# V of layer A transposed as pairs of bf16 in float32 words: three transposes a quad in place of six

## The chip, the cores and the metric

The kernel runs on one core of one Trainium2 chip. The metric is device time in microseconds of the whole program; the kernel before has a median of 3122.47 us in three runs (3122.36 to 3126.64). The engines are named as in the profile: PE is TensorE (PEld its weight loads), DVE is VectorE, ACT is ScalarE, POOL is GpSimd, SP is SyncE.

## The reference

Two layers alternate, A, B, A, B, on a sequence of 2048 positions with 640 features, each with a layer norm ahead of it and a residual. Layer A is attention with a recurrent memory: the sequence is cut into 64 segments of 32, each segment is put behind 8 memory rows, and the memory of the next segment is the output of the memory rows of this one. So the segments of one A layer follow one another strictly. It has 32 heads of 192 features:

```
mem = mem0
for s in range(n_seg):
    h = concatenate([mem, x[:, s*32:(s+1)*32]])       # 40 rows
    q, k, v = h @ Wq, h @ Wk, h @ Wv                  # 32 heads of 192
    p = softmax(where(mask, q k^T * 192**-0.5, -1e9))
    o = (p v) @ Wo
    mem = o[:, :8]; outs.append(o[:, 8:])
```

Layer B is attention with 32 heads of 20 features, in which a position sees itself and the positions 2, 4, ..., 14 before it (a band mask on two segments of 32: the current one and the one before).

## The kernel before, in words

Everything is held feature-major: features on partitions, positions in the free dimension. Two lanes run side by side, lane 0 the first pair of layers (A, B), lane 1 the second pair, two segments behind, so that one pass over layer A's weights serves 2 x 40 = 80 columns (NT). `step(t)` (L822) is one segment of both lanes; there are 67 steps, the first and last two with one lane alone, and the last one only finishes layer B. Layer B of the step before is woven into the step of layer A.

A step has eight quads of four heads (768 features, six pieces of 128). For each quad PE computes K, Q and V with thirty matmuls each (`proj`, L286, the matmul at L297: 6 pieces x 5 chunks of 640), evacuated by ACT (K, L309 to L311) and DVE (Q to `QT` at L316, V to `vT` at L342). V comes out feature-major and is needed row-major, so `a_vt` (L344) transposes its six pieces on PE (L351; 128 columns each, so that neighbouring columns come along and are not used) into one PSUM bank as bf16, and DVE copies 768 columns of 80 rows to `Vt` (L353). `Vt` has columns of ones beside the values, which give the sums of the softmax. `a_s` (L356) makes the scores and ACT their exponentials `E` (L366); `a_mask` (L369) multiplies by the mask on DVE; `a_pv` (L375) computes `ps_o` from `E` and `Vt` in eight matmuls (L384), ACT takes Ln and Exp of the sums to get `R` (L388, L390), and `a_norm` (L393) multiplies on DVE into `OT` (L398 to L400). `a_o` (L403, L415) adds the quad's thirty matmuls with Wo to the accumulator `ps_acc`, five quads later than the quad's Q, K and V.

The order on every engine is written out by hand in `step` (L829 to L910), under a manual schedule, and each engine takes its own instructions in that order. In quad i of the loop PE has: K of quad i, the transposes of V of quad i-1, Q of quad i, PV of quad i-1, V of quad i, from quad 5 on an `a_o`, then the scores of quad i. DVE has, in the same order: the copy to `Vt` of quad i-1, `QT` of quad i, `vT` of quad i, `OT` of quad i-1, the mask of quad i. Behind the loop the last quad gets its own order, in which the copy stands ahead of the mask (L882 to L884). Layer B's pieces lie between: `b_mask` (L590) multiplies `EB` with a band mask on DVE (L594), `b_vt` (L551) transposes its V (L555) and copies it to `VB` (L559), `b_norm` (L610) divides. `b_qexp` (L561) spreads the queries over heads on POOL (`QX`, L566), which also makes the sums of the layer norm of the next step (L438 and L448 to L461).

PSUM tiles have names by bank: `ps_v`, `ps_vt` share bank 2, `ps_q` and `ps_s` bank 1, `ps_k` and `ps_bq` bank 0. `ps_o` has two banks of its own.

Weights of 41 of 64 halves stay in SBUF; the other 23 are streamed each step by SP through a ring of four buffers (L221 to L251). SBUF is nearly full of them; `hT`, `KF`, `Kz` and `vT` have pads at their ends, because weight loads and transposes read 128 columns where 80 are meant.

The first band masks are built on POOL in the prologue (`build_masks_b`, L186): `maskB[0]` and `maskB[1]` for even and odd segments, and two more with one block cleared for the first segment of each lane (`maskB_first`), for which there is no segment before.

Of the kernel before, what the change touches and what calls it, by code (L numbers as in the profile page):

```python
# [10 lines left out]
BF16 = mybir.dt.bfloat16  # L11
F32 = mybir.dt.float32
ACT = mybir.ActivationFunctionType
ALU = mybir.AluOpType
# [64 lines left out]
class Kernel:  # L79
# [34 lines left out]
    def build_consts(self):  # L114
# [2 lines left out]
        ident = cp.tile([P, P], BF16, name="ident")  # L117
        make_identity(nc, ident[:])
        self.ident = ident
        eps_t = cp.tile([P, 1], F32, name="eps_t")  # L120
        nc.vector.memset(eps_t[:], EPS)
        self.eps_t = eps_t
# [13 lines left out]
        self.xin = pers("xin", [P, 2, NC, SEG], 2, zero=False)  # L136
        self.x_load(0)

        self.hT = pers("hT", [P, NC * NT + 88], 1)[0]
        self.KF = pers("KF", [P, 4 * NT + 48], 1)[0]  # L140
        self.Kz = pers("Kz", [P, 4 * NT + 48], 1)[0]
        self.Vt = pers("Vt", [P, 2 * VH], 1, zero=False)[0]
        nc.vector.memset(self.Vt[:], 1.0)
        self.vT = pers("vT", [P, 6 * NT + 48], 1)[0]
        nc.vector.memset(self.xin[0][:, 1], 0.0)
        nc.vector.memset(self.xin[1][:], 0.0)
        self.h2T = pers("h2T", [P, NC, NX], 1, zero=False)[0]
# [24 lines left out]
    def build_mask_a(self):  # L172
# [10 lines left out]
                                    base=-c0, pattern=[[0, LT]], channel_multiplier=1)  # L183
        self.maskA = mA

    def build_masks_b(self):  # L186
        nc, cp = self.nc, self.cp

        def band(name, cur):
            m = cp.tile([P, NX], BF16, name=name)  # L190
            nc.gpsimd.memset(m[:], 0.0)
            for half in range(2):
                off = 0 if half == cur else SEG
                for l in range(2):
                    r0 = 64 * half + SEG * l
                    blk = m[r0:r0 + SEG, SEG * l:SEG * (l + 1)]
                    for w in range(BW):
                        nc.gpsimd.affine_select(out=blk, in_=blk, compare_op=ALU.not_equal, fill=1.0,
                                                base=off - BDIL * w, pattern=[[1, SEG]], channel_multiplier=-1)
            return m  # L200

        self.maskB = [band("mB0", 0), band("mB1", 1)]
        f0 = cp.tile([P, NX], BF16, name="mB_f0")
        nc.gpsimd.tensor_copy(out=f0[:], in_=self.maskB[0][:])
        nc.gpsimd.memset(f0[64:64 + SEG, :], 0.0)
        f1 = cp.tile([P, NX], BF16, name="mB_f1")
        half1 = 1 - LAG % 2
        nc.gpsimd.tensor_copy(out=f1[:], in_=self.maskB[LAG % 2][:])
        nc.gpsimd.memset(f1[64 * half1 + SEG:64 * half1 + 2 * SEG, :], 0.0)
        self.maskB_first = {0: f0, LAG: f1}  # L210

        self.hmask = []
        for c, (h0, h1) in enumerate(B_HEADS):
            n, off = h1 - h0, P * c - BD * h0
            hm = cp.tile([P, n], BF16, name=f"hmask{c}")
            nc.gpsimd.memset(hm[:], 1.0)
            nc.gpsimd.affine_select(out=hm[:], in_=hm[:], compare_op=ALU.is_ge, fill=0.0, base=off, pattern=[[-BD, n]], channel_multiplier=1)
            nc.gpsimd.affine_select(out=hm[:], in_=hm[:], compare_op=ALU.is_ge, fill=0.0, base=BD - 1 - off, pattern=[[BD, n]], channel_multiplier=-1)
            self.hmask.append(hm)
# [115 lines left out]
    def a_v(self, i, t):  # L335

        self.v_rows = self.one_lane() and not 2 <= i <= 3
        if self.v_rows:
            return self.a_v_rows(i, t)
        nc = self.nc  # L340
        ps = self.proj("v", i, t)
        nc.vector.tensor_copy(out=self.cols(self.vT[:, 0:6 * NT].rearrange("p (a n) -> p a n", a=6)), in_=self.cols(ps[:, 0:6 * NT].rearrange("p (a n) -> p a n", a=6)))  # L342

    def a_vt(self):  # L344

        if self.v_rows:
            return
        nc = self.nc
        ps = self.ps_big.tile([P, 6, P], BF16, name="ps_vt", tag="bank2")
        for n in range(6):  # L350
            nc.tensor.transpose(out=ps[:, n, :], in_=self.vT[:, NT * n:NT * n + P], identity=self.ident[:])  # L351
        vt = self.Vt
        nc.vector.tensor_copy(out=vt[0:NT, :].rearrange("p (a b c) -> p a b c", a=2, b=2)[:, :, :, 0:DH],  # L353
                              in_=ps[0:NT].rearrange("p (a b) c -> p a (b c)", a=2).rearrange("p a (b c) -> p a b c", b=2))

    def a_s(self):  # L356
        nc = self.nc
# [17 lines left out]
    def a_pv(self):  # L375


        nc = self.nc
        em, vt = self.em, self.Vt
        ops = self.ps_two.tile([P, 2, 512], F32, name="ps_o", tag="o")  # L380
        ov = ops[:, :, 0:4 * NT].rearrange("p a (k n) -> p a k n", k=4)
        for pr in range(2):
            for k, c0 in enumerate((0, 128, 192, 320)):
                nc.tensor.matmul(self.cols(ov[:, pr, k]), lhsT=vt[0:NT, VH * pr + c0:VH * pr + c0 + P], rhs=self.cols(em[0:NT, 2 * pr + k // 2]), start=True, stop=True)  # L384
        r = self.ap1.tile([P, 2, 2, NT], F32, name="R")
        for j, src in ((0, ov[64:P, :, 1]), (1, ov[0:64, :, 2])):
            for r0 in (0, 64):
# [201 lines left out]

    def b_mask(self, b, g):  # L590
        e = self.ebs[g]
        mask = self.maskB_first.get(b, self.maskB[b % 2])
        n = self.on.stop - self.on.start
        self.nc.vector.tensor_tensor(out=e[:, :, self.on], in0=e[:, :, self.on], in1=mask[:, self.on].unsqueeze(1).to_broadcast([P, BG, n]), op=ALU.mult)  # L594

# [226 lines left out]
    def step(self, t):  # L822
# [6 lines left out]
        for i in range(NQUAD - 1):  # L829
# [34 lines left out]
                self.b_s(2 * i - 3)  # L864
            if b is not None and i == 6:
                self.b_wo(b)
            if i == 1:
                if nt < self.n_seg:
                    self.x_load(nt)
# [119 lines left out]
```

## Time and profile before

| | |
|---|---|
| runs, median (lowest to highest) | 3122.47 us (3122.36 to 3126.64) |
| profiled execution, span | 3128.7 us |
| mean granted TensorE clock over the span | 0.993 |
| PE instructions of the transposes of V (L351) | 3024 matmuls, 504 groups of six |
| DVE copies to Vt (L353) | 504, 279.0 us in all |
| DVE casts to vT (L342) | 504, 329.3 us in all |
| HBM read and written | 770.22 MB, 2.62 MB |

The page gives one time for the profiled execution, its span from the first to the last instruction; it is 1.002 times the median of the runs. Every row of a timeline has the start in us from the span's start, the length, the engine, the line of the kernel, the operation, what it writes and reads, the sizes, and how many equal instructions are merged; in brackets stands how long the engine was idle ahead of it and what ended that. A row of a group has the count, the busy time and the mean of one in ns, then the idle time ahead of them with what ended most of it. Matmuls overlap, so the time that PE spends on a group is read from its start to the start of the next group, not from the length in its row.

### The profile page before, as it was taken

What the parts mean: (1) busy time and instruction counts of PE and PEld (TensorE: products, weight loads), DVE (VectorE), ACT (ScalarE), POOL (GpSimd) and SP (SyncE); (2) the same over time, 40 slices, a digit from 0 to 9 for tenths busy, and PEclk for the clock granted to TensorE, in tenths of its full rate; (3) what the DMA queues carried; (4) which work ended last, traced back from release to release, by engine and by line L of the source; (5) the groups of instructions that cost most, each with busy time, mean ns of one, the idle gap of its engine ahead of it and who ended that gap; (6) DMA issues with size and microseconds to landing.
All of it is one profiled execution on the core that took longest, in us unless ns stands there. A gap on an engine that the chain in (4) does not pass through costs nothing.

```text
span 3128.7 us, 187179 instructions
## 1 busy us (share of the span) xinstructions
PE 3079.1 (98%) x83454; PEld 3030.8 (97%) x83454; DVE 2369.5 (76%) x6009; ACT 1845.1 (59%) x5612; POOL 553.2 (18%) x1028
## 2 busy tenths in 40 slices
PE   6999999999999999999999999999999999999998
PEld 4899999999999999999999999999999999999997
DVE  3677777777777777777777777777777777877776
ACT  2556656656656656656656656656656656655654
POOL 2111111111111111111111111111111111111121
PEclk7999999999999999999999999999999999999999
DMA  9877777777777777777777777777777777777776
GB/s 392 287 246 248 246 246 239 250 243 246 249 244 249 246 246 250 247 247 247 247 246 248 248 245 249 250 246 245 250 246 248 249 244 249 250 243 250 248 251 219
DMA packets 452970, 785.02 MB, mean 251 GB/s; under 512 B 58560, under 2 KB 444352, under 8 KB 452160
## 3 DMA queue, kind: packets, MB, share of 16 engines
q1 hardware_dynamic: 438480, 767.84, 76.4%
q8 instruction: 652, 10.68, 1.4%
q10 hardware_dynamic: 13680, 5.21, 0.7%
q14 instruction: 158, 1.29, 0.1%
HBM read 770.22 MB, written 2.62 MB: 247 GB/s over the span
## 4 chain that ended last, share of the span: by engine, by line
PE 96%; DMA 3%; issue 1%; ACT 0%; DVE 0%; SPq 0%; ACTq 0%
PE ps_k L297 18%; PE ps_acc L415 18%; PE ps_q L297 17%; PE ps_v L297 17%; PE ps_vt L351 5%; PE ps_o L384 5%; PE ps_s L363 2%; PE ps_s L364 2%; PE ps_bs L581 2%; PE ps_bk L529 2%; PE ps_by L640 2%; PE ps_bq L529 1%; PE ps_bv L529 1%; PE ps_vr L331 1%; PE ps_bo L607 1%
## 5 line engine op out<-in xcount | busy, mean ns | idle before, releaser
L388 ACT ACTIVATE R<-ps_o 64x160 f32<-64x160 f32 (+1 forms) x2112 | 620.1, 294 | 338.4 <-PE ps_o L384 122.8
L297 PEld LDWEIGHTS <-w_ring 128*128 128x128 bf16 x16470 | 676.6, 100 | 18.7 <-issue 5.3
L297 PE MATMUL ps_q<-hT,w_q 128*128 128x80 bf16 (+1 forms) x12870 | 541.1, 201 | 4.8 <-DMA w_q<-in_A_Wq_dram 4.2
L566 POOL TENSOR_TENSOR QX<-QB,hmask 128x448 bf16<-128x448 bf16 (+2 forms) x325 | 304.5, 945 | 1338.2 <-ACT QB L544 1025.1
L297 PEld LDWEIGHTS <-w_q 128*128 128x128 bf16 x12870 | 493.8, 100 | 6.0 <-DMA w_q<-in_A_Wq_dram 5.3
L309 ACT CAST KF<-ps_k 128x320 bf16<-128x320 f32 (+1 forms) x528 | 218.5, 414 | 414.7 <-PE ps_k L297 399.1
L415 PE MATMUL ps_acc<-OT,w_o 128*128 128x80 bf16 (+1 forms) x9900 | 458.9, 201 | 3.7 <-DMA w_o<-in_A_Wo_dram 2.3
L342 DVE CAST vT<-ps_v 128x480 bf16<-128x480 f32 (+1 forms) x504 | 329.3, 653 | 166.2 <-PE ps_v L297 148.1
L316 DVE CAST QT<-ps_q 128x480 bf16<-128x480 f32 (+1 forms) x528 | 337.5, 639 | 119.7 <-PE ps_q L297 116.5
L297 PE MATMUL ps_v<-hT,w_v 128*128 128x80 bf16 (+1 forms) x9480 | 423.7, 201 | 4.1 <-issue 2.4
L415 PEld LDWEIGHTS <-w_o 128*128 128x128 bf16 x9900 | 393.2, 100 | 5.4 <-DMA w_o<-in_A_Wo_dram 2.9
L297 PE MATMUL ps_k<-hT,w_k 128*128 128x80 bf16 (+1 forms) x7920 | 373.5, 201 | 2.9 <-DMA w_k<-in_A_Wk_dram 2.7
L297 PEld LDWEIGHTS <-w_v 128*128 128x128 bf16 x9480 | 371.6, 100 | 4.9 <-issue 2.9
L297 PE MATMUL ps_k<-hT,w_ring 128*128 128x80 bf16 (+1 forms) x7860 | 370.5, 201 | 5.4 <-issue 3.4
L366 ACT ACTIVATE E<-ps_s 80x320 bf16<-80x320 f32 (+1 forms) x528 | 220.7, 418 | 241.4 <-PE ps_s L364 240.1
L398 DVE TENSOR_TENSOR OT<-ps_o,R 128x320 bf16<-128x320 f32 (+1 forms) x528 | 254.1, 481 | 135.4 <-ACT R L390 115.7
L297 PEld LDWEIGHTS <-w_k 128*128 128x128 bf16 x7920 | 321.5, 100 | 3.7 <-DMA w_k<-in_A_Wk_dram 3.1
L353 DVE COPY Vt<-ps_vt 80x768 bf16<-80x768 bf16 x504 | 279.0, 554 | 56.4 <-PE ps_vt L351 44.5
L415 PE MATMUL ps_acc<-OT,w_ring 128*128 128x80 bf16 (+1 forms) x5940 | 307.9, 201 | 1.5 <-issue 1.1
L297 PE MATMUL ps_v<-hT,w_ring 128*128 128x80 bf16 (+1 forms) x5640 | 264.8, 202 | 0.8 <-DMA w_ring<-in_A_Wv_dram 0.7
L372 DVE TENSOR_TENSOR E<-E,maskA 80x320 bf16<-80x320 bf16 (+1 forms) x528 | 207.0, 392 | 64.7 <-ACT E L366 54.0
L390 ACT ACTIVATE R<-R 128x320 f32<-128x320 f32 (+1 forms) x528 | 244.1, 462 | 16.7
(159 smaller groups left out, 4932.2 us busy)
## 6 DMA issues: line engine op xcount, KB each, us to landing
w_ring<-in_A_Wk_dram SPq DMA_DIRECT2D x1036, 240.0 KB, 3.7
w_ring<-in_A_Wo_dram SPq DMA_DIRECT2D x780, 240.0 KB, 3.8
w_ring<-in_A_Wv_dram SPq DMA_DIRECT2D x776, 240.0 KB, 4.0
w_ring<-in_A_Wq_dram SPq DMA_DIRECT2D x390, 240.0 KB, 4.0
w_q<-in_A_Wq_dram SPq DMA_DIRECT2D x5, 960.0 KB, 11.0
w_v<-in_A_Wv_dram SPq DMA_DIRECT2D x6, 480.0 KB, 11.3
w_ring<-in_A_Wk_dram SPq DMA_DIRECT2D x6, 480.0 KB, 10.2
w_ring<-in_A_Wo_dram SPq DMA_DIRECT2D x6, 480.0 KB, 11.3
```

What stands on the lines that cost most here:

```text
L297: nc.tensor.matmul(ps[:, NT * n + self.c0:NT * n + self.c1], lhsT=w[n // 3][:, c, P * (n % 3):P * (n % 3 + 1)], rhs=hT[:, NT * c + self.c0 ...
L309: nc.scalar.copy(out=kf, in_=pv[:, :, 0:3:2, :])
L316: self.nc.vector.tensor_copy(out=self.cols(qt[:]), in_=self.cols(ps[:, 0:6 * NT].rearrange("p (a n) -> p a n", a=6)))
L342: nc.vector.tensor_copy(out=self.cols(self.vT[:, 0:6 * NT].rearrange("p (a n) -> p a n", a=6)), in_=self.cols(ps[:, 0:6 * NT].rearrange("p ...
L353: nc.vector.tensor_copy(out=vt[0:NT, :].rearrange("p (a b c) -> p a b c", a=2, b=2)[:, :, :, 0:DH], in_=ps[0:NT].rearrange("p (a b) c -> p ...
L366: nc.scalar.activation(out=self.cols(e[0:NT]), in_=self.cols(sv[0:NT]), func=ACT.Exp, scale=float(DH) ** -0.5)
L372: nc.vector.tensor_tensor(out=self.cols(e[0:NT]), in0=self.cols(e[0:NT]), in1=self.cols(self.maskA[0:NT, :]).unsqueeze(1).to_broadcast([NT ...
L388: nc.scalar.activation(out=self.cols(r[r0:r0 + 64, :, j]), in_=self.cols(src), func=ACT.Ln)
L390: nc.scalar.activation(out=rf, in_=rf, func=ACT.Exp, scale=-1.0)
L398: nc.vector.tensor_tensor(out=oc[:, :, 0:3:2], in0=ov[:, :, 0:4:3], in1=r, op=ALU.mult)
L415: nc.tensor.matmul(self.cols(acc[:, k]), lhsT=w[m // 3][:, m % 3, P * c:P * (c + 1)], rhs=self.cols(ot[:, m]), start=(i == 0 and m == 0 an ...
L566: self.nc.gpsimd.tensor_tensor(out=qx[:, 0:nh, self.on], in0=self.qb[:, c, self.on].unsqueeze(1).to_broadcast([P, nh, n]), in1=self.hmask[ ...
```

## The change

A transpose moves 32-bit words in place of bf16. For that, the cast from `ps_v` to `vT` writes the piece n of the quad's first pair of heads and piece n of its second pair side by side, so that two bf16 make one float32 word; `vT` is then read as float32 of 3 x 80 columns, and three transposes of 80 columns against a float32 identity (`ident4`) write 80 rows of 3 x 128 words. The copy from PSUM to `Vt` reads those words as bf16 and parts the pairs: its source has a step of two elements, its destination is as before. PE's weight loads of these transposes are no instructions of their own in the program: the float32 matmul brings its own. The order of the work on PE, DVE, ACT and SP is the same as before, instruction by instruction, but for the three transposes.

The second identity takes room in SBUF, which comes from the pads of `hT` and `vT` and from the two masks for first segments. `maskB[0]` is now built without its block of the segment before; the first segment of each lane uses it so, and the block of that lane is filled in place by eight selects on POOL at quad 6 of that step (steps 1 and 3).

```diff
--- before.py
+++ after.py
@@ -117,6 +117,9 @@
         ident = cp.tile([P, P], BF16, name="ident")
         make_identity(nc, ident[:])
         self.ident = ident
+        ident4 = cp.tile([P, P], F32, name="ident4")
+        make_identity(nc, ident4[:])
+        self.ident4 = ident4
         eps_t = cp.tile([P, 1], F32, name="eps_t")
         nc.vector.memset(eps_t[:], EPS)
         self.eps_t = eps_t
@@ -136,12 +139,12 @@
         self.xin = pers("xin", [P, 2, NC, SEG], 2, zero=False)
         self.x_load(0)
 
-        self.hT = pers("hT", [P, NC * NT + 88], 1)[0]
+        self.hT = pers("hT", [P, NC * NT + 48], 1)[0]
         self.KF = pers("KF", [P, 4 * NT + 48], 1)[0]
         self.Kz = pers("Kz", [P, 4 * NT + 48], 1)[0]
         self.Vt = pers("Vt", [P, 2 * VH], 1, zero=False)[0]
         nc.vector.memset(self.Vt[:], 1.0)
-        self.vT = pers("vT", [P, 6 * NT + 48], 1)[0]
+        self.vT = pers("vT", [P, 2 * BG * SEG], 1)[0]
         nc.vector.memset(self.xin[0][:, 1], 0.0)
         nc.vector.memset(self.xin[1][:], 0.0)
         self.h2T = pers("h2T", [P, NC, NX], 1, zero=False)[0]
@@ -183,31 +186,27 @@
                                     base=-c0, pattern=[[0, LT]], channel_multiplier=1)
         self.maskA = mA
 
+    def band_block(self, m, half, cur, l):
+
+        r0 = 64 * half + SEG * l
+        blk = m[r0:r0 + SEG, SEG * l:SEG * (l + 1)]
+        for w in range(BW):
+            self.nc.gpsimd.affine_select(out=blk, in_=blk, compare_op=ALU.not_equal, fill=1.0,
+                                         base=(0 if half == cur else SEG) - BDIL * w, pattern=[[1, SEG]], channel_multiplier=-1)
+
     def build_masks_b(self):
         nc, cp = self.nc, self.cp
 
         def band(name, cur):
             m = cp.tile([P, NX], BF16, name=name)
             nc.gpsimd.memset(m[:], 0.0)
-            for half in range(2):
-                off = 0 if half == cur else SEG
-                for l in range(2):
-                    r0 = 64 * half + SEG * l
-                    blk = m[r0:r0 + SEG, SEG * l:SEG * (l + 1)]
-                    for w in range(BW):
-                        nc.gpsimd.affine_select(out=blk, in_=blk, compare_op=ALU.not_equal, fill=1.0,
-                                                base=off - BDIL * w, pattern=[[1, SEG]], channel_multiplier=-1)
+            for l in range(2):
+                self.band_block(m, cur, cur, l)
             return m
 
         self.maskB = [band("mB0", 0), band("mB1", 1)]
-        f0 = cp.tile([P, NX], BF16, name="mB_f0")
-        nc.gpsimd.tensor_copy(out=f0[:], in_=self.maskB[0][:])
-        nc.gpsimd.memset(f0[64:64 + SEG, :], 0.0)
-        f1 = cp.tile([P, NX], BF16, name="mB_f1")
-        half1 = 1 - LAG % 2
-        nc.gpsimd.tensor_copy(out=f1[:], in_=self.maskB[LAG % 2][:])
-        nc.gpsimd.memset(f1[64 * half1 + SEG:64 * half1 + 2 * SEG, :], 0.0)
-        self.maskB_first = {0: f0, LAG: f1}
+        for l in range(2):
+            self.band_block(self.maskB[1], 0, 1, l)
 
         self.hmask = []
         for c, (h0, h1) in enumerate(B_HEADS):
@@ -339,19 +338,20 @@
             return self.a_v_rows(i, t)
         nc = self.nc
         ps = self.proj("v", i, t)
-        nc.vector.tensor_copy(out=self.cols(self.vT[:, 0:6 * NT].rearrange("p (a n) -> p a n", a=6)), in_=self.cols(ps[:, 0:6 * NT].rearrange("p (a n) -> p a n", a=6)))
+        nc.vector.tensor_copy(out=self.cols(self.vT[:, 0:6 * NT].rearrange("p (b n a) -> p a b n", b=3, a=2)),
+                              in_=self.cols(ps[:, 0:6 * NT].rearrange("p (a b n) -> p a b n", a=2, b=3)))
 
     def a_vt(self):
 
         if self.v_rows:
             return
         nc = self.nc
-        ps = self.ps_big.tile([P, 6, P], BF16, name="ps_vt", tag="bank2")
-        for n in range(6):
-            nc.tensor.transpose(out=ps[:, n, :], in_=self.vT[:, NT * n:NT * n + P], identity=self.ident[:])
-        vt = self.Vt
-        nc.vector.tensor_copy(out=vt[0:NT, :].rearrange("p (a b c) -> p a b c", a=2, b=2)[:, :, :, 0:DH],
-                              in_=ps[0:NT].rearrange("p (a b) c -> p a (b c)", a=2).rearrange("p a (b c) -> p a b c", b=2))
+        ps = self.ps_big.tile([P, 3, P], F32, name="ps_vt", tag="bank2")
+        vT = self.vT[:, 0:6 * NT].bitcast(F32)
+        for n in range(3):
+            nc.tensor.transpose(out=ps[0:NT, n, :], in_=vT[:, NT * n:NT * (n + 1)], identity=self.ident4[:])
+        nc.vector.tensor_copy(out=self.Vt[0:NT, :].rearrange("p (a b c) -> p a b c", a=2, b=2)[:, :, :, 0:DH],
+                              in_=ps[0:NT].rearrange("p b c -> p (b c)").bitcast(BF16).rearrange("p (b c a) -> p a b c", b=2, a=2))
 
     def a_s(self):
         nc = self.nc
@@ -376,12 +376,12 @@
 
 
         nc = self.nc
-        em, vt = self.em, self.Vt
+        em, vt = self.em, self.Vt[:].rearrange("p (a c) -> p a c", a=2)
         ops = self.ps_two.tile([P, 2, 512], F32, name="ps_o", tag="o")
         ov = ops[:, :, 0:4 * NT].rearrange("p a (k n) -> p a k n", k=4)
         for pr in range(2):
             for k, c0 in enumerate((0, 128, 192, 320)):
-                nc.tensor.matmul(self.cols(ov[:, pr, k]), lhsT=vt[0:NT, VH * pr + c0:VH * pr + c0 + P], rhs=self.cols(em[0:NT, 2 * pr + k // 2]), start=True, stop=True)
+                nc.tensor.matmul(self.cols(ov[:, pr, k]), lhsT=vt[0:NT, pr, c0:c0 + P], rhs=self.cols(em[0:NT, 2 * pr + k // 2]), start=True, stop=True)
         r = self.ap1.tile([P, 2, 2, NT], F32, name="R")
         for j, src in ((0, ov[64:P, :, 1]), (1, ov[0:64, :, 2])):
             for r0 in (0, 64):
@@ -589,7 +589,7 @@
 
     def b_mask(self, b, g):
         e = self.ebs[g]
-        mask = self.maskB_first.get(b, self.maskB[b % 2])
+        mask = self.maskB[b % 2]
         n = self.on.stop - self.on.start
         self.nc.vector.tensor_tensor(out=e[:, :, self.on], in0=e[:, :, self.on], in1=mask[:, self.on].unsqueeze(1).to_broadcast([P, BG, n]), op=ALU.mult)
 
@@ -864,6 +864,8 @@
                 self.b_s(2 * i - 3)
             if b is not None and i == 6:
                 self.b_wo(b)
+            if b in (0, LAG) and i == 6:
+                self.band_block(self.maskB[0], 1, 0, int(b == LAG))
             if i == 1:
                 if nt < self.n_seg:
                     self.x_load(nt)
```

## The prediction

> **What bounds the kernel now.** I read the page's totals first, then the busy time of one step, then the step's timeline engine by engine. From the page:
>
> ```profile
> span 3128.7 us, 187179 instructions
> ...
> PE 3079.1 (98%) x83454; PEld 3030.8 (97%) x83454; DVE 2369.5 (76%) x6009; ACT 1845.1 (59%) x5612; POOL 553.2 (18%) x1028
> ...
> PE 96%; DMA 3%; issue 1%; ACT 0%; DVE 0%; SPq 0%; ACTq 0%
> ```
>
> and from the windows, one step in the middle (start and end, length, then busy time of PE, PEld, DVE, ACT, POOL, granted clock, DMA share, GB/s):
>
> ```profile
> 1541.00:1588.60 47.60, 47.60 (x1299) 47.32 (x1296) 37.01 (x94) 29.21 (x89) 8.23 (x14) 1.00 0.78 248
> ```
>
> PE never rests within a step, at the full granted clock, so a nanosecond saved on PE is a nanosecond of the span, as long as nobody makes PE wait. DVE is busy 37 of 47.6 us. That is an average; what counts is how much earlier DVE delivers than PE asks. The change touches one delivery: the copy of the transposed V (ps_vt to Vt), for which the weight loads of the output products (ps_o, I call them PV) wait. Each step has eight such pairs, quads 1 to 8 below. The copies of this step on DVE (start, length), and the mask behind the last one:
>
> ```profile
> 1541.38 0.55 DVE L353 COPY Vt<-ps_vt 80x768 bf16<-80x768 bf16 x1 [0.27 <-PE ps_vt L351]
> 1547.08 0.55 DVE L353 COPY Vt<-ps_vt 80x768 bf16<-80x768 bf16 x1
> 1552.92 0.55 DVE L353 COPY Vt<-ps_vt 80x768 bf16<-80x768 bf16 x1
> 1557.47 0.55 DVE L353 COPY Vt<-ps_vt 80x768 bf16<-80x768 bf16 x1
> 1561.85 0.55 DVE L353 COPY Vt<-ps_vt 80x768 bf16<-80x768 bf16 x1
> 1567.34 0.56 DVE L353 COPY Vt<-ps_vt 80x768 bf16<-80x768 bf16 x1
> 1573.12 0.55 DVE L353 COPY Vt<-ps_vt 80x768 bf16<-80x768 bf16 x1 [0.32 <-PE ps_vt L351]
> 1577.38 0.55 DVE L353 COPY Vt<-ps_vt 80x768 bf16<-80x768 bf16 x1
> 1577.96 0.32 DVE L372 TENSOR_TENSOR E<-E,maskA 80x320 bf16<-80x320 bf16 x1
> ```
>
> and the PV that takes each, on PE, with the transposes of quad 1 ahead:
>
> ```profile
> 1540.84 0.50 PE L351 MATMUL ps_vt<-ident,vT 128*128 128x128 bf16 x6
> 1541.18 1.24 PE L297 MATMUL ps_q<-hT,w_q 128*128 128x80 bf16 x30
> 1542.25 0.46 PE L384 MATMUL ps_o<-E,Vt 80*128 80x80 bf16 x8
> 1548.82 0.45 PE L384 MATMUL ps_o<-E,Vt 80*128 80x80 bf16 x8
> 1553.73 0.45 PE L384 MATMUL ps_o<-E,Vt 80*128 80x80 bf16 x8
> 1558.11 0.46 PE L384 MATMUL ps_o<-E,Vt 80*128 80x80 bf16 x8
> 1562.46 0.46 PE L384 MATMUL ps_o<-E,Vt 80*128 80x80 bf16 x8
> 1568.05 0.45 PE L384 MATMUL ps_o<-E,Vt 80*128 80x80 bf16 x8
> 1573.99 0.45 PE L384 MATMUL ps_o<-E,Vt 80*128 80x80 bf16 x8
> 1578.42 0.45 PE L384 MATMUL ps_o<-E,Vt 80*128 80x80 bf16 x8
> ```
>
> From copy end to PV start the slack is 0.32, 1.19, 0.26, 0.09, 0.06, 0.15, 0.32 us, and in quad 8 0.14 behind the mask. PE does not wait in any of them, so a hand-over needs at most 0.06. In quads 4 and 5 the kernel is balanced on a knife's edge: PE is full, and DVE is just in time.
>
> **The change, part by part.** The prices come from these groups (count, busy time, mean ns):
>
> ```profile
> L353 DVE COPY Vt<-ps_vt 80x768 bf16<-80x768 bf16 x504 | 279.0, 554 | 56.4 <-PE ps_vt L351 44.5
> L342 DVE CAST vT<-ps_v 128x480 bf16<-128x480 f32 x496 | 326.0, 657 | 159.4 <-PE ps_v L297 141.3
> L342 DVE CAST vT<-ps_v 128x240 bf16<-128x240 f32 x8 | 3.2, 406 | 6.8 <-PE ps_v L297 6.8
> L456 DVE TENSOR_REDUCE ln_s<-sq 128x64 f32<-128x320 bf16 x66 | 46.1, 699 | 0.0
> L351 PE MATMUL ps_vt<-ident,vT 128*128 128x128 bf16 x3024 | 253.4, 220 | 0.3 <-issue 0.2
> ```
>
> *Transposes.* Six occupy PE from 1540.84 to 1541.18, 0.34 us, 57 ns each for 128 streamed columns. Three that stream 128 columns too take 0.17, if a float32 column streams like a bf16 one. No row shows a float32 matmul. Bounds: nothing (a saving of all 0.34), and four times a bf16 one, 0.68. I take 0.17, by the row of the same 128 columns; weight loads of their own could bring it to the old 0.34, which stays in my forecast's range. The Trainium skill ("TensorE: Matmul & The Clock Gate", Terms) says that the transpose mode makes float32 four times faster; by that the sum is the one made here; its section on weight-path modes excludes float32 from fast weight loads, which no run here shows.
>
> *The copy that parts the pairs.* It reads 768 bf16 at every second place in PSUM. The old one reads 768 side by side in 554 ns; the cast at one element per pass takes (657 - 406)/240 = 1.05 ns an element and about 154 ns fixed. 554 - 154 = 400 for 768 is 0.52 ns: the old copy moves two at a time. If the stride stops that, the new one takes 154 + 768 x 1.042 = 0.955 us, 0.40 more. Bounds: 0.554 (rate kept), and the far-strided reads of the sum over chunks, (699 - 154)/320 = 1.70 ns an element, 1.46 us. I take 0.955: the stride here is 4 bytes, not a row. The Trainium skill speaks against the change here: "VectorE: DVE Perf Modes", What auto-detection actually checks, grants two 16-bit elements a cycle only at step one, and its cycle table gives an estimate of (120 + 768)/0.96 = 925 ns. The row of 554 ns agrees with the double rate at step one; no row shows step two.
>
> *The cast to pairs* writes with a step of two elements, but moves one at a time already: 0 taken. By the 1.70 ns row it would cost 0.32 more; ahead of OT in quads 4, 5, 7 and 8 that is up to 1.2 us a step, within the range.
>
> *Masks.* Two selects of eight move into steps 1 and 3 on POOL; two copies and a second half leave the start.
>
> ```profile
> L198 POOL TENSOR_SCALAR_AFFINE_SELECT mB<-mB 32x32 bf16<-32x32 bf16 x64 | 13.3, 212 | 3.4
> L438 POOL TENSOR_TENSOR sq<-xin 128x320 bf16<-128x320 bf16 x65 | 46.7, 719 | 1167.2 <-issue 1053.6 <-DVE xin L646 68.8 <-PE ps_by L640 18.2
> ```
>
> Sixteen selects are 3.4 us, and POOL idles 1167.2/65 = 18 us a step just there: nothing; uncovered, 3.4 us in all. The smaller pads and the second identity cost no time in a step.
>
> **The sum for a step.** The new copy is hidden only where slack is left. d is how much later PV starts than before. How quads 3 to 5 hang together is seen between PV 3 and PV 4, DVE first, then ACT:
>
> ```profile
> 1553.40 0.41 DVE L594 TENSOR_TENSOR EB<-EB,mB 128x512 bf16<-128x512 bf16 x1
> 1553.73 0.65 DVE L316 CAST QT<-ps_q 128x480 bf16<-128x480 f32 x1
> 1554.30 0.55 DVE L559 COPY VB<-ps_bvt 128x320 bf16<-128x320 bf16 x2
> 1554.76 0.41 DVE L594 TENSOR_TENSOR EB<-EB,mB 128x512 bf16<-128x512 bf16 x1
> 1555.30 0.66 DVE L342 CAST vT<-ps_v 128x480 bf16<-128x480 f32 x1
> 1556.03 0.49 DVE L398 TENSOR_TENSOR OT<-ps_o,R 128x320 bf16<-128x320 f32 x1
> 1557.12 0.32 DVE L372 TENSOR_TENSOR E<-E,maskA 80x320 bf16<-80x320 bf16 x1
> ```
> ```profile
> 1553.65 0.60 ACT L587 ACTIVATE EB<-ps_bs 128x512 bf16<-128x512 f32 x1 [0.60 <-PE ps_bs L581]
> 1554.27 1.23 ACT L388 ACTIVATE R<-ps_o 64x160 f32<-64x160 f32 x4
> 1555.53 0.47 ACT L390 ACTIVATE R<-R 128x320 f32<-128x320 f32 x1
> ```
>
> PV, Ln and Exp of the sums on ACT, three OT products, mask, copy, next PV: a ring of 4.38 us with no air. The copy stands in it, so there its whole 0.40 counts, and what PE saves does not.
>
> The walk has two rules. A copy starts at its old time shifted by the d of the PV before it, and by 0.17 less where its row names the transposes as releaser (quads 1 and 7). A PV starts at the later of PE's own arrival (old time, plus d, less 0.17) and the copy's end plus 0.06. Times after 1500:
>
> - Quad 1: copy 41.21 to 42.165, PV 42.225; PE alone would be there at 42.08. d = -0.025.
> - Quad 2: slack; PE arrives at 48.625, the copy ends at 48.01. d = -0.195.
> - Quad 3: copy 52.725 to 53.68, PV 53.74, PE there at 53.365. d = +0.01.
> - Quad 4: DVE comes out of copy 3 0.205 late; the vT cast, which waited 0.13 for PE, starts 0.075 late, and OT still finds R ready when it did, +0.01. Copy 57.48 to 58.435, PV 58.495. d = +0.385.
> - Quad 5: copy 62.235 to 63.19, PV 63.25. d = +0.79.
> - Quad 6: copy 68.13 to 69.085, PV 69.145. d = +1.095.
> - Quad 7: copy 74.045 to 75.00, PV 75.06. d = +1.07.
> - Quad 8: copy 78.45 to 79.405, the mask starts 0.03 later for 0.32, 0.06: PV 79.815. d = +1.395.
>
> From there to the next quad 1 PE is full, so the step carries 1.395 us: PE stands 2.755 us ahead of its PVs and saves 8 x 0.17 = 1.36. Behind a late PV all of PE queues; it takes its matmuls in order. The casts to QT come up to 0.4 later: in quad 3 QT ends near 54.6, while its scores stand behind PV (0.28 us) and thirty V matmuls (1.07 us, as the thirty from 1541.18) that start at 53.74. Bank 2's next writer stands behind PV anyway.
>
> The cast's 496 two-lane instructions, eight a step, make 62 steps: 62 x 1.395 = 86.5 us; the eight one-lane copies add at most 3 and are left out. 3128.7 + 86.5 = 3215.2. The profiled span is 1.002 times the median of the runs, 3122.47; times 0.998 that is **3209 us**.
>
> **Rivals.** The forecast with free transposes, by the same walk, gives d = +0.885, 3177; with transposes as dear as the six, +1.905, 3240.
>
> *The copy keeps its rate* (faster). The same walk with 0.554 gives d = -0.17, -0.34, -0.51, -0.53, -0.53, -0.62, -0.79, -0.87: 62 x -0.87 = -54, **3068**. Quads 4 to 6 gain little even then, the ring sees to that. Between 0.554 and 0.955 the step turns at a copy of 0.71 us. For it: the same bytes. Against it: the operand isn't dense, and the wide rate is seen here on dense runs alone.
>
> *Float32 streams in four passes* (0.68 for three): PE itself is 0.34 later per quad, the ring hides part: d = +3.305, **3327**. Nothing in the trace speaks either way.
>
> *Strided PSUM reads cost as the strided sums do* (1.46 us): d = +4.93, **3428**. Against: 64-byte steps there, 4-byte steps here.
>
> *The change doesn't do what it says*: a copy near 0.71 us cancels the saving, 3122.
>
> **How the numbers follow.** Forecast 0.68, rate kept 0.12, four passes 0.11, slow stride 0.06, cancelled 0.03. The range 3170 to 3330 takes in the forecast's span of 3177 to 3240, the dear cast and four passes; left out are the faster case, the cancelled one and the slow stride, 0.21. A measurement here tells 0.2% from no change, some 6 us: faster 0.12, same 0.04, slower 0.84.
>
> **What would show it.** The copy's mean at 925 to 990 ns, DVE busy near 2369.5 + 504 x 0.40 = 2571 us. Three transposes in 0.17 us from first start to the next matmul. PE idle ahead of PV with Vt as releaser, some 170 us in all, most in quads 4, 5, 6 and 8, none in 2. Casts to pairs at 657. Wrong is the forecast if the copy stays under 0.71, if PE's gap sits at the transposes, or if PE doesn't stand ahead of PV although the copy is long.

## The result, and the profile after

| kernel | median of the runs | span of the profiled execution | ratio to the kernel before, 95% interval |
|---|---|---|---|
| before | 3124.55 us (4 runs, 3122.36 to 3128.65) | 3128.7 us | |
| after | 3238.32 us (4 runs, 3237.59 to 3241.33) | 3235.9 us | 1.0365 [1.0352, 1.0378] |

The change makes the kernel 3.65% slower. These are the page's totals of the changed kernel: the span, the engines' busy times, and the chain that ended last by engine.

```profile
span 3235.9 us, 184156 instructions
...
PE 3143.1 (97%) x81942; PEld 3035.7 (94%) x81942; DVE 2566.7 (79%) x6009; ACT 1848.3 (57%) x5612; POOL 578.6 (18%) x1026
...
PE 55%; DVE 19%; ACT 15%; issue 7%; DMA 3%; SPq 0%; ACTq 0%
```

There are 1512 fewer matmuls, and PE is still 97% busy; the busy shares alone would not tell what happened. The chain does: it was PE for 96% of the span, and now a third of it runs through DVE and ACT. The groups of the changed kernel that answer to those the prediction was priced with (count, busy us, mean ns, then the idle time ahead of them):

```profile
L353 DVE COPY Vt<-ps_vt 80x768 bf16<-80x768 bf16 x504 | 480.6, 954 | 70.7 <-PE ps_vt L352 58.8
L341 DVE CAST vT<-ps_v 128x480 bf16<-128x480 f32 x496 | 349.3, 704 | 185.0 <-PE ps_v L296 181.6
L352 PE MATMUL ps_vt<-ident,vT 128*80 128x128 f32 x1512 | 251.6, 275 | 0.0
L384 PE MATMUL ps_o<-E,Vt 80*128 80x80 bf16 x3968 | 227.2, 203 | 51.6 <-DVE Vt L353 32.0 <-DVE E L372 10.3
L384 PEld LDWEIGHTS <-Vt 80*128 80x128 bf16 x4224 | 179.6, 99 | 114.9 <-DVE Vt L353 79.5 <-issue 16.3
```

The copy went from 554 to 954 ns. Three float32 transposes keep PE's row busy for 251.6 us, where six bf16 ones did for 253.4. And PE now idles ahead of PV (L384), mostly until the copy to Vt. The timeline of PE in the same step as in the prediction shows both, from the transposes of quad 1 and the matmuls behind them to the PVs of quads 4, 5 and 8:

```profile
1541.59 0.50 PE L352 MATMUL ps_vt<-ident,vT 128*80 128x128 f32 x3
1541.92 1.24 PE L296 MATMUL ps_q<-hT,w_q 128*128 128x80 bf16 x30
...
1559.59 0.46 PE L384 MATMUL ps_o<-E,Vt 80*128 80x80 bf16 x8 [0.21 <-DVE Vt L353]
...
1564.35 0.46 PE L384 MATMUL ps_o<-E,Vt 80*128 80x80 bf16 x8 [0.26 <-DVE Vt L353]
...
1581.09 0.45 PE L384 MATMUL ps_o<-E,Vt 80*128 80x80 bf16 x8 [0.16 <-DVE E L372]
```

From the start of the three transposes to the start of the next group pass 0.33 us; for the six it was 0.34. The PVs of quads 4 and 5 stand 4.76 us apart, where they stood 4.35 apart before. DVE's rows of quads 3 and 4 in that step:

```profile
1553.82 0.95 DVE L353 COPY Vt<-ps_vt 80x768 bf16<-80x768 bf16 x1
...
1557.14 0.49 DVE L398 TENSOR_TENSOR OT<-ps_o,R 128x320 bf16<-128x320 f32 x1
...
1558.22 0.32 DVE L372 TENSOR_TENSOR E<-E,maskA 80x320 bf16<-80x320 bf16 x1
1558.58 0.95 DVE L353 COPY Vt<-ps_vt 80x768 bf16<-80x768 bf16 x1
```

The copy of quad 4 ends at 1559.53, and its PV starts 0.06 later. From the copy of quad 3 to that of quad 4 it is 4.76 us as well. The ring that the prediction read between PV 3 and PV 4 took 4.38: it is the same ring, with 0.40 more in the copy and 0.02 less elsewhere. In quads 3 and 6 the rows of PV's matmuls name no wait, but those of its weight loads do:

```profile
1554.82 0.33 PEld L384 LDWEIGHTS <-Vt 80*128 80x128 bf16 x8 [0.22 <-DVE Vt L353]
...
1570.24 0.33 PEld L384 LDWEIGHTS <-Vt 80*128 80x128 bf16 x8 [0.32 <-DVE Vt L353]
```

**Where in a step the time goes.** The starts of the transposes of quads 1 to 8 cut a step into eight intervals; the interval n to n+1 holds the PV of quad n. The table gives the median of each over the 61 intervals of two-lane steps, in us, worked out from the starts in the traces, for the two kernels and for those experiments (below) in which it is needed.

| interval | before | after | e1 | e2 | e6 | e9 | e11 |
|---|---|---|---|---|---|---|---|
| 1 to 2 | 5.595 | 5.737 | 5.742 | 5.592 | 5.595 | 5.714 | 5.708 |
| 2 to 3 | 5.356 | 5.352 | 5.356 | 5.353 | 5.356 | 5.417 | 5.417 |
| 3 to 4 | 4.906 | 5.125 | 5.122 | 4.902 | 4.907 | 5.679 | 5.067 |
| 4 to 5 | 4.137 | 4.513 | 4.514 | 4.134 | 4.518 | 4.134 | 4.133 |
| 5 to 6 | 5.633 | 6.038 | 6.035 | 5.636 | 6.034 | 5.612 | 5.613 |
| 6 to 7 | 6.109 | 6.426 | 6.424 | 6.106 | 6.109 | 6.105 | 6.105 |
| 7 to 8 | 4.137 | 4.279 | 4.283 | 4.135 | 4.137 | 4.134 | 4.133 |
| 8 to 1 | 10.840 | 11.155 | 11.150 | 10.835 | 10.839 | 10.835 | 10.835 |
| whole step | 46.716 | 48.629 | 48.629 | 46.692 | 47.496 | 47.633 | 47.019 |

A step of the changed kernel is 1.913 us longer in the median. In the mean it is 1.78 (48.639 against 46.859), because some steps of the kernel before are drawn out, up to 47.76 us; 61 x 1.78 = 108.6 us, and the spans differ by 107.2.

### The profile page after: what moved, and what is told of

Read it like the earlier page. It is cut to its first block, busy times and chain, and to the rows that moved or that the text cites. A ratio compares the mean times of both kernels' runs of the same rounds, so it can differ in the third digit from the quotient of the medians.

```text
span 3235.9 us, 184156 instructions
## 1 busy us (share of the span) xinstructions
PE 3143.1 (97%) x81942; PEld 3035.7 (94%) x81942; DVE 2566.7 (79%) x6009; ACT 1848.3 (57%) x5612; POOL 578.6 (18%) x1026
## 4 chain that ended last, share of the span: by engine, by line
PE 55%; DVE 19%; ACT 15%; issue 7%; DMA 3%; SPq 0%; ACTq 0%
PE ps_acc L415 12%; PE ps_k L296 9%; ACT R L388 9%; PE ps_v L296 9%; PE ps_q L296 8%; DVE Vt L353 7%; PE ps_o L384 5%; ACT R L390 3%; DVE E L372 3%; DVE OT L400 2%; DVE OT L399 2%; DVE OT L398 2%; PE ps_vt L352 2%; PE ps_bk L529 1%; PE ps_by L640 1%
## 5 line engine op out<-in xcount | busy, mean ns | idle before, releaser
L566 POOL TENSOR_TENSOR QX<-QB,hmask 128x448 bf16<-128x448 bf16 (+2 forms) x325 | 329.8, 1023 | 1392.5 <-ACT QB L544 1080.5
L353 DVE COPY Vt<-ps_vt 80x768 bf16<-80x768 bf16 x504 | 480.6, 954 | 70.7 <-PE ps_vt L352 58.8
L296 PEld LDWEIGHTS <-w_q 128*128 128x128 bf16 x12870 | 507.1, 100 | 9.7 <-DMA w_q<-in_A_Wq_dram 6.0
L341 DVE CAST vT<-ps_v 128x480 bf16<-128x480 f32 (+1 forms) x504 | 352.7, 700 | 192.6 <-PE ps_v L296 189.1
L384 PE MATMUL ps_o<-E,Vt 80*128 80x80 bf16 (+1 forms) x4224 | 239.2, 201 | 53.4 <-DVE Vt L353 33.7
L384 PEld LDWEIGHTS <-Vt 80*128 80x128 bf16 x4224 | 179.6, 99 | 114.9 <-DVE Vt L353 79.5
```

Of the source, the lines that this page charges most:

```text
L296: nc.tensor.matmul(ps[:, NT * n + self.c0:NT * n + self.c1], lhsT=w[n // 3][:, c, P * (n % 3):P * (n % 3 + 1)], rhs=hT[:, NT * c + self.c0 ...
L353: nc.vector.tensor_copy(out=self.Vt[0:NT, :].rearrange("p (a b c) -> p a b c", a=2, b=2)[:, :, :, 0:DH], in_=ps[0:NT].rearrange("p b c -> ...
L384: nc.tensor.matmul(self.cols(ov[:, pr, k]), lhsT=vt[0:NT, pr, c0:c0 + P], rhs=self.cols(em[0:NT, 2 * pr + k // 2]), start=True, stop=True)
L566: self.nc.gpsimd.tensor_tensor(out=qx[:, 0:nh, self.on], in0=self.qb[:, c, self.on].unsqueeze(1).to_broadcast([P, nh, n]), in1=self.hmask[ ...
```

## The experiments

The theory under test: the whole loss is the 0.40 us by which the copy is longer, in a ring in which PE waits for DVE, and the transposes give nothing back. The rivals: the float32 transposes or their weight loads cost PE time, the stepped cast costs it, or the masks do. A ratio here is always to the kernel before on the same chip.

### e1: the slow copy alone

The kernel before, with its six bf16 transposes and its cast, in which only the copy's source takes every second element. In this kernel, and in e5 and e6, V's features therefore come out in another order.

```diff
-                              in_=ps[0:NT].rearrange("p (a b) c -> p a (b c)", a=2).rearrange("p a (b c) -> p a b c", b=2))
+                              in_=ps[0:NT].rearrange("p n c -> p (n c)").rearrange("p (b c a) -> p a b c", b=2, a=2))
```

> The kernel before with its six bf16 transposes, its cast and its masks; only the copy to Vt reads every second place, as the changed kernel does, so the features of V come out in another order. Theory (the copy, 0.40 us longer, stands in the ring from PV to PV, and three float32 transposes occupy PE as long as six): copy 0.954 us and about 3233 us, within 8 us of the changed kernel's 3238. Rival (the float32 transposes themselves, or the cast to pairs, are the loss): the copy gets longer but the time stays within 30 us of 3124.

Measured: 3239.69 us, ratio 1.0356 [1.0342, 1.0371]. Its groups of the copy, the transposes, and PV's weight loads:

```profile
L353 DVE COPY Vt<-ps_vt 80x768 bf16<-80x768 bf16 x504 | 480.7, 954 | 74.4 <-PE ps_vt L351 62.5
...
L351 PE MATMUL ps_vt<-ident,vT 128*128 128x128 bf16 x3024 | 253.4, 220 | 0.0
...
L384 PEld LDWEIGHTS <-Vt 80*128 80x128 bf16 x4224 | 179.6, 99 | 113.7 <-DVE Vt L353 78.5 <-issue 16.0
```

One edit alone gives the time of the whole change, nearly the same idle time ahead of PV (113.7 against 114.9 us), and in the table the changed kernel's step interval by interval, none off by more than 5 ns. On top of the slow copy, all the rest of the change, the three transposes in place of six among it, neither adds nor saves anything.

### e2: the change without the slow copy

The changed kernel, in which the pairs stay side by side in Vt: the copy is dense, and PV's weight loads read every second column instead.

```diff
-        nc.vector.tensor_copy(out=self.Vt[0:NT, :].rearrange("p (a b c) -> p a b c", a=2, b=2)[:, :, :, 0:DH],
-                              in_=ps[0:NT].rearrange("p b c -> p (b c)").bitcast(BF16).rearrange("p (b c a) -> p a b c", b=2, a=2))
+        nc.vector.tensor_copy(out=self.Vt[0:NT, :].rearrange("p (b e) -> p b e", b=2)[:, :, 0:2 * DH],
+                              in_=ps[0:NT].rearrange("p b c -> p (b c)").bitcast(BF16).rearrange("p (b e) -> p b e", b=2))
...
-        em, vt = self.em, self.Vt[:].rearrange("p (a c) -> p a c", a=2)
+        em, vt = self.em, self.Vt[:].rearrange("p (c a) -> p a c", a=2)
```

> The changed kernel with its three float32 transposes and its cast to pairs, but the pairs stay together in Vt: the copy reads and writes side by side, and the weight loads of PV step over every second column. Theory: copy back at 0.55 us, the transposes still 0.33 us for three, the time back at 3124 us within 8. Rival (float32 transposes or the cast): still within 20 of 3238. If stepped weight loads cost PE time, the intervals of the eight PV matmuls show it, 0.28 us before.

Measured: 3124.98 us in 11 runs, ratio 0.9989 [0.998, 0.9997]. The copy, the transposes, and PV's weight loads with their step of two:

```profile
L353 DVE COPY Vt<-ps_vt 80x768 bf16<-80x768 bf16 x504 | 279.2, 554 | 54.4 <-PE ps_vt L352 42.4
L352 PE MATMUL ps_vt<-ident,vT 128*80 128x128 f32 x1512 | 251.5, 275 | 0.0
...
L384 PEld LDWEIGHTS <-Vt 80*128 80x128 bf16 x4224 | 186.7, 98 | 6.9 <-DVE Vt L353 0.9 <-issue 0.2
```

With the copy at 554 ns again the loss is gone, and so is PE's wait, though the float32 transposes, the cast to pairs and the masks are all there. This is also the change without its flaw, and it gains 0.11%: the interval ends just under 1, and the gain is less than the 0.2% named in the prediction as what can be told from no change. PE is full in it, so what three float32 transposes save against six bf16 ones can be read directly: they take 0.334 us in place of 0.337, which makes 0.024 us a step in the table, 1.5 us in all. The weight loads with a step of two take 98 ns, and those of the changed kernel, with a step of one, 99. The Trainium skill ("TensorE: Matmul & The Clock Gate", Weight-path perf modes) lists steps between weight columns among what fast weight loads allow, and this agrees.

### e3: what a float32 transpose costs

The changed kernel with three transposes added, whose results nobody reads, each behind one of the three: in quad 1 of the same shape (80 weight columns, 128 streamed), in quad 2 with 32 weight columns, in quads 6 and 7 with 64 rows in and 64 columns streamed (80 and 32 weight columns).

```diff
+        m, k = {1: (NT, P), 2: (32, P), 6: (NT, 64), 7: (32, 64)}.get(self.nvt, (0, 0))
...
+            if m:
+                nc.tensor.transpose(out=ps[0:m, 3, 0:k], in_=vT[0:k, NT * n:NT * n + m], identity=self.ident4[0:k, 0:k])
```

> The changed kernel with three more float32 transposes, into a fourth quarter of the bank that nobody reads, in quads 1 (80 weight columns, 128 streamed), 2 (32 and 128), 6 (80 and 64) and 7 (32 and 64). What they add on PE tells what sets 0.11 us a transpose. If the streamed columns at half the bf16 rate do: 0.33, 0.33, 0.17, 0.17 us in that order. If the loading of float32 weight columns does: 0.33, 0.13, 0.33, 0.13. The time itself isn't the question; it rises by some tens of us at most.

Measured in one run: 3358.26 us. From the first of the six to the next group the medians over 62 steps are 661 ns in quad 1 and 662 in quad 2, against 334 for three. The timeline of one quad 2, PE and its weight loads (PEld):

```profile
1503.10 0.12 PEld L354 LDWEIGHTS ps_vt<-ident,vT 128*80 128x80 f32 x1
1503.13 0.28 PE L354 MATMUL ps_vt<-ident,vT 128*80 128x128 f32 x1
1503.13 0.10 PEld L356 LDWEIGHTS ps_vt<-ident,vT 128*32 128x32 f32 x1
1503.24 0.27 PE L356 MATMUL ps_vt<-ident,vT 128*32 128x128 f32 x1
1503.25 0.12 PEld L354 LDWEIGHTS ps_vt<-ident,vT 128*80 128x80 f32 x1
1503.35 0.27 PE L354 MATMUL ps_vt<-ident,vT 128*80 128x128 f32 x1
```

One starts every 0.11 us, twice the 56 ns of a bf16 one (six in 337 ns), whether its weights have 80 columns or 32 (their loads take 0.12 and 0.10). So the number of weight columns does not set the pace, and what is left among the things varied or shared here is the 128 float32 columns that both stream, at half the rate of bf16. A kernel that streams fewer columns without changing the rows was not run, so the rate per streamed column is the reading, not a measurement of its own.

The expectation failed in quads 6 and 7. There the six take 1231 and 1164 ns, and the time rose by 120 us over the changed kernel. A quad 6:

```profile
1524.48 0.28 PE L354 MATMUL ps_vt<-ident,vT 128*80 128x128 f32 x1
...
1524.69 0.11 PEld L356 LDWEIGHTS ps_vt<-ident,vT 64*80 64x80 f32 x1
1524.69 0.25 PE L356 MATMUL ps_vt<-ident,vT 64*80 64x64 f32 x1
1524.87 0.12 PEld L354 LDWEIGHTS ps_vt<-ident,vT 128*80 128x80 f32 x1
1524.87 0.31 PE L354 MATMUL ps_vt<-ident,vT 128*80 128x128 f32 x1
```

In quad 2 the weights of the next transpose load as the one ahead of it starts (both at 1503.13). Here a load starts only with its own matmul, and a pair of 128 and 64 rows takes 0.41 us instead of 0.22. The smaller transposes are dearer than the larger ones; which of rows, streamed columns or their alternation is at fault was not tried.

### e4 and e7: the masks, and the cast to pairs

e4 is the kernel before with the edit of the masks alone. e7 adds the cast to pairs, and lets six bf16 transposes read them with a step of two:

```diff
-        nc.vector.tensor_copy(out=self.cols(self.vT[:, 0:6 * NT].rearrange("p (a n) -> p a n", a=6)), in_=self.cols(ps[:, 0:6 * NT].rearrange("p (a n) -> p a n", a=6)))
+        nc.vector.tensor_copy(out=self.cols(self.vT[:, 0:6 * NT].rearrange("p (b n a) -> p a b n", b=3, a=2)),
+                              in_=self.cols(ps[:, 0:6 * NT].rearrange("p (a b n) -> p a b n", a=2, b=3)))
...
-            nc.tensor.transpose(out=ps[:, n, :], in_=self.vT[:, NT * n:NT * n + P], identity=self.ident[:])
+            nc.tensor.transpose(out=ps[:, n, :], in_=self.vT[:].rearrange("p (n a) -> p a n", a=2)[:, n // 3, NT * (n % 3):NT * (n % 3) + P], identity=self.ident[:])
```

> The kernel before with the masks of the changed kernel alone: built in place, no masks for first segments. Theory and forecast: nothing, 3124.5 within 4 us. Rival (the selects on POOL in steps 1 and 3 or the new prologue hold something up): up to some 10 us more, all of it in the first four steps.

> The kernel before with the new masks and with the cast that lays V down in pairs; six bf16 transposes read their weights at every second place, and the copy is dense as before. Theory: the cast takes 0.70 us in place of 0.66, and the time stays at 3124 within 6, since the cast has 0.07 us of room ahead of OT in the tight quads. Rival (the cast is part of the loss): 10 to 25 us more. If stepped weight loads cost PE time, the six transposes take longer than 0.34 us.

Measured: e4 3125.36 us, ratio 1.0001 [0.9992, 1.001]; e7 3123.9 us, ratio 0.9999 [0.999, 1.0008]. The cast of e7:

```profile
L338 DVE CAST vT<-ps_v 128x480 bf16<-128x480 f32 x496 | 349.3, 704 | 158.0 <-PE ps_v L293 139.8
```

The step of two in its destination makes the cast 704 ns long instead of 657, but DVE has idle time ahead of it (158 us, most of it until PE's V), and the time does not move. Both edits cost nothing.

### e5 and e6: the slow copy in two quads at a time

As e1, but only in quads 1 and 2 (e5) or 4 and 5 (e6); the other six copies are dense.

```diff
+                              in_=parted if self.nvt in (4, 5) else dense)
```

> The kernel before, with the copy that reads every second place in quads 1 and 2 alone (features of V in another order there). Theory (slack by quad): quad 1 has 0.32 of slack for 0.40 plus a hand-over of 0.06, quad 2 has 1.19, so PV comes 0.145 us later a step: 9 us less what of the ring's waits for weights it covers, 3124 to 3134. Rival (DVE's load as such costs, wherever it lies): a quarter of the whole loss, 28 us, 3153.

> The kernel before, with the copy that reads every second place in quads 4 and 5 alone (features of V in another order there): as much DVE time as in quads 1 and 2. Theory: +0.375 in quad 4 and +0.405 in quad 5, none of it given back, 0.78 us a step, 48 us less up to 9 that weight waits gave before: 3164 to 3173. Rival (DVE's load as such): 28 us, 3153, the same as for quads 1 and 2.

Measured: e5 3132.68 us, ratio 1.0028 [1.0019, 1.0037], 8.7 us more; e6 3171.6 us, ratio 1.0149 [1.0136, 1.0163], 47.7 us more. Both kernels make the same number of slow copies, and the same DVE time is added; where DVE has slack it costs little, and in the ring all of it counts. In e6 the intervals 4 to 5 and 5 to 6 grow by 0.381 and 0.401 us, all others by nothing: 61 x 0.78 = 47.7 us. PE's waits in e6 (us in total, times, longest):

```profile
PEld L387 <- DVE Vt L356: 45.1, 128, 0.7
...
PE ps_o L387 <- DVE Vt L356: 29.8, 127, 0.6
```

Some 128 waits in 62 steps are two a step, those of the two quads. The two rows are two views of the same waits, and are not to be added.

### e8: half of the copy on ACT

The changed kernel, with the copy split between DVE and ACT, one head of each pair for either, ahead of ACT's three K copies.

```diff
+        nc.vector.tensor_copy(out=out[:, :, 0, 0:DH], in_=src[:, :, 0])
+        nc.scalar.copy(out=out[:, :, 1, 0:DH], in_=src[:, :, 1])
```

> The changed kernel with the copy shared: the first 384 features of each row by DVE, the other 384 by ACT, which does its part ahead of the three copies of K. Theory (the copy's length in the ring is the loss): DVE's part takes 0.55 us as the whole copy did before, ACT's about 0.46, and the time goes back to 3124 to 3140 us. Rival (transposes or cast): it stays within 20 of 3238.

Measured: 3392.14 us, ratio 1.0844 [1.0828, 1.0861]: far off. The reason stands in the list of waits and in the two groups:

```profile
ACT Vt L360 <- DVE Vt L359: 693.2, 493, 3.3
```
```profile
L359 DVE COPY Vt<-ps_vt 80x384 bf16<-80x384 bf16 x504 | 278.5, 553 | 66.1 <-PE ps_vt L356 56.3
L360 ACT COPY Vt<-ps_vt 80x384 bf16<-80x384 bf16 x504 | 239.0, 474 | 709.9 <-DVE Vt L359 693.2 <-DMA xin<-in_A_x_dram 10.7 <-DMA out_dram<-YT 6.1
```

ACT's half waited for DVE's in 493 of 504 copies: the halves ran one behind the other, 553 + 474 ns in the ring, and K's copies behind them. The expectation speaks of the first and the last 384 features, but the edit gives either engine one head of each pair, so the halves lie between one another in Vt; whether that is why one waits for the other was not tried. As a test of the theory it is void: the ring became longer instead of shorter.

### e9, e10 and e11: the whole copy on ACT

e9 moves the whole parting copy to ACT, ahead of the K copies; e10 does the same to the dense copy of the kernel before.

```diff
-        nc.vector.tensor_copy(out=self.Vt[0:NT, :].rearrange("p (a b c) -> p a b c", a=2, b=2)[:, :, :, 0:DH],
+        nc.scalar.copy(out=self.Vt[0:NT, :].rearrange("p (a b c) -> p a b c", a=2, b=2)[:, :, :, 0:DH],
...
             if i >= 1:
                 self.a_vt()
+            self.a_k_out()
```

> The changed kernel, with the whole parting copy moved from VectorE to ScalarE, ahead of ScalarE's three K copies. Theory (the copy's length in VectorE's round of a quad is the loss, and TensorE waits for it): ScalarE needs about 0.78 us for the copy by its shorter parts in e8 (474 ns for 384 columns, so some 0.17 us and 0.79 ns a column), VectorE's round loses 0.95 us, the copy no longer queues behind the scores' work, TensorE is full again, and the time is 3120 to 3135 us. Rival one (the loss lies in the three float32 transposes or in the cast): within 20 us of 3238. Rival two (ScalarE's exponentials come later by the copy and the round through ScalarE becomes the longer one): 3140 to 3200.

> The kernel before, with its dense copy of V moved from VectorE to ScalarE, ahead of the three K copies. Theory (TensorE is full before the change, and VectorE's round hides in it): no gain though VectorE is relieved by 0.55 us a quad, 3124 us within 8. Rival (VectorE's round bounds the kernel before as well): faster by over 10 us.

Measured: e9 3184.02 us, ratio 1.0171 [1.0157, 1.0185]; e10 3188.26 us, ratio 1.0185 [1.0171, 1.0198]. Neither came out as the theory had it. Rival two of e9 has the right size, but not the right place, as the groups of e9 show (PE's matmuls of layer B's scores, the copy, and PV):

```profile
L585 PE MATMUL ps_bs<-QX,KB 128*128 128x256 bf16 x124 | 33.6, 271 | 37.5 <-ACT Kz L314 37.5
```
```profile
L357 ACT COPY Vt<-ps_vt 80x768 bf16<-80x768 bf16 x504 | 398.9, 792 | 298.7 <-PE ps_vt L356 289.9 <-DMA w_ring<-in_A_Wk_dram 0.9
...
L388 PE MATMUL ps_o<-E,Vt 80*128 80x80 bf16 (+1 forms) x4224 | 236.7, 199 | 0.7 <-ACT Vt L357 0.2
```

PV no longer waits for Vt (0.2 us in all). What PE waits for is Kz: ACT idles ahead of the copy until the transposes are done, the K copies stand behind it, and in quad 3 layer B's scores write the bank (0) that the K copies still read. e10 has the same wait (38.0 us on the same shape), and no parting copy, so this loss belongs to the move and not to the change. The table shows it in one interval: 3 to 4, 0.77 us longer in e9. And the five intervals from 4 to 5 on to 8 to 1, in which the changed kernel loses 0.376 + 0.405 + 0.317 + 0.142 + 0.315 = 1.56 us a step, are all back at or under those of the kernel before, with the float32 transposes and the stepped cast in place. e11 was made to see the rest go: as e9, with quad 3 left as in the changed kernel.

```diff
+        copy = nc.vector.tensor_copy if i == 3 else nc.scalar.copy
...
+            if i == 3:
+                self.a_k_out()
             if i >= 1:
                 self.a_vt(i)
+            if i != 3:
+                self.a_k_out()
```

> As e9, but in quad 3 the parting copy stays on VectorE and the K copies keep their place. In e9 TensorE no longer waited for V (0.4 us in all), and its loss of about 60 us stood in one interval of a step, from the transposes of quad 3 to those of quad 4 (5.68 us, where the kernel before has 4.91), where layer B's scores reuse the bank that ScalarE's late K copies still read; quads 1 and 2 lost another 0.18 us. Theory (the long copy in VectorE's round is the whole loss of the change, and what is left in e9 is that bank): the 0.77 us x 61 = 47 us go, and with 0.18 x 61 = 11 us left the time is 3125 to 3142 us. Rival (the float32 transposes or the stepped cast carry part of the loss of the change): it stays above 3160.

Measured: 3144.19 us, ratio 1.0051 [1.0037, 1.0064], 2 us above the range of the theory and 16 below the rival's bound. The kernel before took 3129.86 us on that chip, so 14.3 us are left of the 114 that the change costs. 0.303 us a step are left over the kernel before: 0.161 in interval 3 to 4, where the copy of 954 ns stands on DVE once more and PV waits for it, 61 times:

```profile
PEld L389 <- DVE Vt L358: 10.3, 61, 0.5
```

and 0.113 and 0.061 in the intervals 1 to 2 and 2 to 3, as in e9 and about as in e10; what in the move costs these was not followed further.

No kernel of these beats the kernel before by the 0.2% that the prediction asks for; e2 comes nearest, with 0.11%.

## Why the prediction was right, and where it was off

The forecast was 3209 us, and 3238.3 was measured: slower, as forecast, inside the range, and 29 us above the forecast itself.

- *PE full, DVE just in time in quads 4 and 5*: right. e6 adds 0.40 us to each of these two copies, and gets 0.38 and 0.40 on the step.
- *The copy, 0.955 us because a step of two stops the double rate*: right, 954 ns. With the 154 ns that the prediction took as fixed, that is 1.04 ns an element, the rate of the cast. The estimate that the prediction worked out from the Trainium skill ("VectorE: DVE Perf Modes"), 925 ns, is 3% short.
- *Three transposes in 0.17 us, "if a float32 column streams like a bf16 one"*: the term that was mis-sized. They take 0.334 us, the six took 0.337. Bounds and forecast span held it (the old 0.34, by which the walk gives +1.905 a step and 3240 us), but I chose the nearest row in shape, which was of another type. That the time lies in the range is owed to these bounds, and not to the 0.17. The reason that the prediction gave for the dear case, weight loads of their own, is not what e3 shows: its pace does not change with the weights' width. As for the sentence of the Trainium skill that transpose mode makes float32 four times faster ("TensorE: Matmul & The Clock Gate", Terms): every float32 matmul of these runs is a transpose, so there is none outside that mode to compare with, and these transposes go at half the pace of the bf16 ones. By that rule alone the sum could not be made.
- *The walk through the quads*: right. With 0.34 for the transposes its d is 0.145, 0.145, 0.35, 0.725, 1.13, 1.435, 1.58, 1.905; the table's differences between after and before add up to 0.142, 0.138, 0.357, 0.733, 1.138, 1.455, 1.597, 1.912. As predicted the delay starts anew in each quad but the second, and PE never catches up.
- *From the step to the time*: 62 x 1.905 = 118 us by the dear walk, and the spans differ by 107.2. Some 8 of the 11 us between are in the kernel before: its mean step is 0.14 us above the median, that of the changed kernel 0.01, which makes 0.13 x 61. What draws out its single steps was not tried, nor were the other 3 us followed.
- *PE's idle time ahead of PV, some 170 us, with Vt as releaser*: 114.9 on its weight loads, 79.5 of them with Vt as releaser. The 170 are 62 x 2.755, the delay of a step together with the time by which faster transposes would have brought PE there earlier. They saved nothing, and by the walk with 0.34 it is 62 x 1.905 = 118 us. In the step shown the waits stand in quads 3, 4, 5, 6 and 8, and none in 2, as said (those of 3 and 6 in the rows of the weight loads alone, shown with the result). In quads 1 and 7 the intervals grow by 0.142 each and no wait is listed: the modelled end of the matmuls ahead (1541.92 + 1.24 = 1543.16) lies behind PV's start (1543.13), and hides it.
- *The cast at 657, 0 taken*: it takes 704, and costs nothing (e7). *Masks 0*: right (e4). DVE's busy time came to 2566.7 us, with 2571 predicted, and that is luck: the groups of the copy and the cast grew by 201.6 and 23.3 us, and the total grew by only 197.2, because it counts time in which two of DVE's rows overlap once.
- *Two side sums*: by the prediction's two rules as they stand, four passes come to +3.11 a step and 3315 us, not +3.305 and 3327, and the step turns at a copy of 0.73 us, not 0.71. Neither moves the forecast or the range.

That the ring would hide most of PE's own saving was part of the forecast: of 1.36 us a step, the walk lets 0.51 through (1.395 against 1.905). It could not be seen, since there was no saving to speak of.

## What to carry to other kernels

Price a copy by its access pattern and not by its bytes: parting pairs at the evacuation on DVE cost 0.40 us for each 768 elements, while letting the weight loads of the next matmul take every second column cost nothing. Look for the ring in which the consumer waits for the copy before counting what PE saves: the same 0.40 us in two quads of each step was worth 9 us in all where there was slack and 48 us where there was none. And before halving the number of instructions with a wider type, measure one of them: here each took twice as long.

## What the runs showed of the hardware beyond that

- A float32 transpose with 128 rows and 128 streamed columns starts every 0.11 us, with 80 or with 32 weight columns; a bf16 one every 56 ns.
- Where float32 transposes of 128 rows and 128 streamed columns alternate with such of 64 and 64, a weight load starts only with its own matmul, and a pair takes 0.41 us (0.39 with 32 weight columns in the smaller one) against 0.22.
- A cast from float32 in PSUM whose bf16 destination has a step of two takes 704 ns instead of 657 for 480 elements.
- ACT parts the same 768 elements in 792 ns, and copies them dense in 792 ns too (e9 and e10): there the step costs nothing, while DVE goes from 554 to 954.
